# Time mixing with a SoLU expert on one core: w in pairs, w_out in place, halves added before their column sums, masks first, and a second instruction order

## Chip, cores and metric

One core of a Trainium2 chip. The metric is the device time of one execution in microseconds (us); lower is better. Every run is an execution of the whole kernel. An execution that is over 1.5% above the fastest of its kernel counts as slow and is left out of the ratios. A profile belongs to one execution; its span, from the first instruction recorded to the last, is about 1.8 us shorter than the time of that execution.

## The reference

The first half is a recurrence over time with a state of 48 x 48 per head; the second half takes its output, token by token, through two matrices with an exp-weighted activation and a layer norm between.

```python
# r, k, v, w: (4, 8, 768, 48) f32;  u: (8, 48)
for t in range(S):
    cur = einsum('bhd,bhe->bhde', u * k[t], v[t])
    y[t] = einsum('bhd,bhde->bhe', r[t], state + cur)
    state = w[t][..., None] * state + einsum('bhd,bhe->bhde', k[t], v[t])
x = y as (3072, 384)
h = x @ w_in                       # (3072, 1024)
e = exp(h - max(h));  solu = h * e / sum(e)
ln = (solu - mean) / sqrt(var + 1e-6) * g_ln
out = ln @ w_out                   # (3072, 384)
```

## The kernel before

The work is cut into 24 units of 128 tokens (6 chunks of time for each of 4 batches). A unit passes through some forty stages, each a short function. One long list, `ORDER`, says in which order the stages of all units are written into the program: the word `es13v` is stage `es` of unit 13 on VectorE (`a` ScalarE, `v` VectorE, `g` GpSimd). Each engine runs its own words strictly in the order of that list, so a word that waits holds up every later word of its engine.

Names that matter: `ldw ldk ldr ldv` load, `lw` is log w, `cum` its cumulated sums, `H` the hidden product, `e` its exp, `he` = h e, `hq` = (h e) squared, `Oa` and `Ob` the halves of the output product, `sq qm lv rs` the small chain that makes the norm's factor, `o` the scaled output, `sto` its store. `dm` are filler matmuls. SBUF is the core's working memory; PSUM is the memory that TensorE's results go to, and tiles that end in `_ps` lie there. To evict a tile is to copy it out of PSUM.

```python
# loads: one unit, one tensor, 192 KB
t = io.tile([C, H, 64], F32, tag=name + "_in", ...)            # 7 buffers
sp.dma_start(out=L[name], in_=src[b, :, c * C:(c + 1) * C, :].rearrange("h t d -> t h d"))
...
def log_w(i):
    act.activation(out=L["lw"][:, :, :D], in_=L["w"], func=LN)
...
# w_out: gains into gw, then the mean of the rows subtracted into w2
engine.tensor_scalar(out=gw[:, f, :], in0=wout_f[:, f, :], scalar1=gr[:, f:f + 1], op0=MULT, ...)
engine.tensor_add(out=w2[:, f, :DM], in0=gw[:, f, :], in1=mean_sb)
...
def output(i, part):               # o_ps: (128, 387), columns 385 and 386 are the two sums
    for f in range(part * KF // 2, (part + 1) * KF // 2):
        pe.matmul(o_ps[:, :DM + 1], lhsT=he[:, f, :], rhs=w2[:, f, :], ...)
        pe.matmul(o_ps[:, DM + 1:DM + 2], lhsT=e[:, f, :], rhs=inv_col, ...)
    if part == 1:
        for f in range(KF):        # KF = 8
            pe.matmul(o_ps[:, DM + 2:], lhsT=L["hq"][:, f, :], rhs=one_col, ...)
...
L["o"] = io.tile([C, DM], F32, tag="o", name="o", bufs=5)
```

The end of its list, from unit 23's x on:

```text
X23 qm19 lv19 hq20g o19a xT22v e21 xT23v H22 e22 he21 Ob20 sto18 hq21g sq20a qm20 lv20 H23 he22 Oa21
Oa22 sto19 Ob21 e23 hq22g sq21a o20v qm21 lv21 Ob22 he23 hq23v Oa23 sto20 sq22v sq23a qm22 o21v Ob23
sto21 lv22 qm23 Oc23 o22v sto22 lv23 dm14 oz23v dm15 o23a stz23 dm7 sto23 dm11 dm19
```

The softmax here doesn't subtract the row's maximum and nothing guards it: scores larger than these inputs give would overflow.

## Time and profile before

| | time, us |
|---|---|
| median of the first three runs | 151.97 (151.48 to 153.03) |
| the execution that was profiled (slow) | 156.91, span 155.2 |
| a later profile (`before_again`) | 151.62, span 149.8 |

The profile fell into a slow execution; the prediction below reads that one, and it infers that a fast execution has almost no idle time of TensorE after 35 us. The second profile was taken with the experiments.

### The profile page before, as it was taken

What the parts mean: (1) busy time and instruction counts of PE and PEld (TensorE: products, weight loads), DVE (VectorE), ACT (ScalarE), POOL (GpSimd) and SP (SyncE); (2) the same over time, 40 slices, a digit from 0 to 9 for tenths busy, and PEclk for the clock granted to TensorE, in tenths of its full rate; (3) what the DMA queues carried; (4) which work ended last, traced back from release to release, by engine and by line L of the source; (5) the groups of instructions that cost most, each with busy time, mean ns of one, the idle gap of its engine ahead of it and who ended that gap; (6) DMA issues with size and microseconds to landing.
All of it is one profiled execution on the core that took longest, in us unless ns stands there. A gap on an engine that the chain in (4) does not pass through costs nothing.

```text
span 155.2 us, 5295 instructions
## 1 busy us (share of the span) xinstructions
PE 140.4 (90%) x2156; PEld 109.7 (71%) x2156; DVE 129.4 (83%) x231; ACT 120.2 (77%) x232; POOL 123.1 (79%) x152
## 2 busy tenths in 40 slices
PE   6877897699999899999999799939999999999993
PEld 2344584477786787888788587737888778889771
DVE  7546738899998898999976989999889999998661
ACT  4456767989898979798989698829899888895742
POOL 3375965997999799999947999977799899976800
PEclk9999999999999999999999999999999999999999
DMA  4999997989999999899796999999989311011013
GB/s 95 201 185 301 380 303 152 213 160 190 208 202 184 204 229 187 194 205 233 154 205 157 218 217 200 228 250 180 215 196 211 100 51 55 2 55 55 18 62 127
DMA packets 104970, 27.09 MB, mean 175 GB/s; under 512 B 100329, under 2 KB 104562, under 8 KB 104946
## 3 DMA queue, kind: packets, MB, share of 16 engines
q1 hardware_dynamic: 104946, 26.75, 76.4%
q8 instruction: 17, 0.28, 0.7%
q14 instruction: 7, 0.06, 0.1%
HBM read 22.03 MB, written 4.72 MB: 172 GB/s over the span
## 4 chain that ended last, share of the span: by engine, by line
PE 50%; DMA 14%; DVE 10%; SPq 8%; POOL 8%; ACT 4%; issue 3%; POOLq 0%; DVEq 0%
PE o_ps L71 18%; PE h_ps L71 13%; SPq L71 8%; DMA kr_in<-in_k_dram 8%; DMA wout_f<-in_moe_w_out_dram 6%; POOL w L71 5%; PE kr_ps L71 5%; PE cum_ps L71 3%; PE m_ps L71 3%; PE y_ps L71 3%; PE s_ps L71 3%; DVE hq L71 3%; DVE kp L71 2%; PE x_ps L71 2%; DVE he L71 1%
## 5 line engine op out<-in xcount | busy, mean ns | idle before, releaser
L71 PE MATMUL o_ps<-w,he 128*128 128x385 bf16 (+2 forms) x200 | 42.2, 315 | 0.3 <-ACT sq L71 0.3
L71 PE MATMUL h_ps<-xT,win_sb 128*128 128x128 bf16 x576 | 36.0, 219 | 0.1
L71 PEld LDWEIGHTS <-win_sb 128*128 128x128 bf16 x576 | 32.9, 98 | 0.9 <-issue 0.2
L71 PE MATMUL o_ps<-inv_col,e 128*128 128x1 bf16 x192 | 31.1, 165 | 0.0
L71 DVE TENSOR_TENSOR he<-h_ps,e 128x1024 bf16<-128x1024 f32 x24 | 29.2, 1217 | 2.2 <-ACT e L71 2.2
L71 POOL TENSOR_TENSOR hq<-he 128x1024 bf16<-128x1024 bf16 x14 | 26.5, 1895 | 3.7 <-DVE he L71 2.4
L71 ACT ACTIVATE e<-h_ps 128x1024 bf16<-128x1024 f32 x24 | 24.5, 1021 | 6.2 <-PE h_ps L71 6.1
L71 PEld LDWEIGHTS <-he 128*128 128x128 bf16 x208 | 19.7, 96 | 10.5 <-issue 0.3
L71 ACT ACTIVATE cum_ps<-cum_ps 128x772 f32<-128x772 f32 (+1 forms) x24 | 19.2, 801 | 8.8 <-PE cum_ps L71 7.6
L71 DVE TENSOR_TENSOR kp<-cum_ps,kr_in 128x768 bf16<-128x768 f32 x24 | 22.7, 948 | 0.6 <-DMA kr_in<-in_r_dram 0.5
L71 POOL TENSOR_TENSOR q<-p,u_bc 128x384 bf16<-128x384 bf16 x23 | 22.0, 962 | 0.6 <-DVE p L71 0.5
L71 POOL TENSOR_TENSOR p<-kr_in 128x384 bf16<-128x384 f32 x18 | 17.9, 1001 | 5.4 <-DMA kr_in<-in_k_dram 5.4
L71 PEld LDWEIGHTS <-kp 128*128 128x128 bf16 x272 | 17.6, 102 | 4.4 <-DVE kp L71 2.3
L71 POOL TENSOR_TENSOR dv<-vb,dg 128x384 bf16<-128x384 bf16 x22 | 18.2, 830 | 2.3 <-ACT vb L71 1.5
L71 DVE TENSOR_TENSOR m<-m_ps,uts 128x1024 bf16<-128x1024 f32 x14 | 17.0, 1223 | 3.1 <-PE m_ps L71 3.0
L71 PEld LDWEIGHTS <-e 128*128 128x128 bf16 x192 | 18.3, 96 | 0.1
L71 PE MATMUL kr_ps<-ident,kp 128*128 128x128 bf16 x192 | 15.9, 230 | 1.4 <-DVE kp L71 1.4
L71 PEld LDWEIGHTS <-kr 64*128 64x128 bf16 (+1 forms) x272 | 10.7, 98 | 4.9 <-DVE kr L71 2.2
L71 ACT ACTIVATE lw<-w_in 128x384 bf16<-128x384 f32 x23 | 11.7, 523 | 2.7 <-DMA w_in<-in_w_dram 2.7
L71 ACT COPY kr<-kr_ps 128x1024 bf16<-128x1024 bf16 x13 | 13.2, 1014 | 0.5 <-PE kr_ps L71 0.4
L71 POOL TENSOR_SCALAR_AFFINE_SELECT m<-m 128x1024 bf16<-128x1024 bf16 x10 | 11.0, 1103 | 2.5 <-ACT m L71 2.4
L71 PE MATMUL cum_ps<-lw,uti_neg 128*128 128x384 bf16 x24 | 8.3, 347 | 4.8 <-DVE kp L71 3.3
(93 smaller groups left out, 284.3 us busy)
## 6 DMA issues: line engine op xcount, KB each, us to landing
w_in<-in_w_dram SPq DMA_DIRECT2D x24, 192.0 KB, 4.2
kr_in<-in_r_dram SPq DMA_DIRECT2D x24, 192.0 KB, 3.8
kr_in<-in_k_dram SPq DMA_DIRECT2D x24, 192.0 KB, 3.8
v_in<-in_v_dram SPq DMA_DIRECT2D x24, 192.0 KB, 3.8
out_dram<-o SPq DMA_DIRECT2D x23, 192.0 KB, 3.1
win_f<-in_moe_w_in_dram SPq DMA_DIRECT2D x3, 512.0 KB, 6.1
wout_f<-in_moe_w_out_dram SPq DMA_DIRECT2D x2, 768.0 KB, 8.8
out_dram<-o SPq DMA_DIRECT2D x2, 96.0 KB, 1.6
```

The costliest lines, as they stand in the source:

```text
L71: made = make(*args, **kwargs)
```

## The change

The intent: fewer instructions (w of two units loaded and logged at once from unit 4 on; half of the one-column matmuls of some units replaced by one addition of halves), less memory (w_out scaled in place), an earlier identity mask, and a list in a second order that fits the new durations. The queue of loads is nearly as it was. Cut to its core:

```diff
+ t2 = io.tile([C, 2, H, 64], F32, tag="w_in", name="w_in", bufs=4)          # load, name == "w"
+ if i >= 4:
+     sp.dma_start(out=L["w2_in"]..., in_=src[b:b + 2, :, c * C:(c + 1) * C, :]...)
- act.activation(out=L["lw"][:, :, :D], in_=L["w"], func=LN)
+ act.activation(out=<both units of t>, in_=<both units of w2_in>, func=LN)   # i >= 4
- engine.tensor_scalar(out=gw[:, f, :], in0=wout_f[:, f, :], ...)
+ engine.tensor_scalar(out=w2[:, f, :DM], in0=wout_f[:, f, :], ...)
- engine.tensor_add(out=w2[:, f, :DM], in0=gw[:, f, :], in1=mean_sb)
+ engine.tensor_add(out=w2[:, f, :DM], in0=w2[:, f, :DM], in1=mean_sb)
+ def halves(name, of):                     # es from e, hs from hq; 12 uses
+     t = L[name] = wk.tile([128, KF // 2, C], BF16, tag=name, name=name, bufs=2)
+     engine.tensor_add(out=t, in0=L[of][:, :KF // 2, :], in1=L[of][:, KF // 2:, :])
+ hq = L.get("hs", L["hq"]);  n = hq.shape[1]           # 4 matmuls where halves were added, else 8
+ # the sums of the second half of e are now a word of their own, Oe, left out where es exists
+ # masks: uti_neg, ident, uts, ident_f in one loop ahead of all else on GpSimd
```

The list is written anew in full. Its end now reads:

```text
X23 sto17 lv19 e22 xT23v es21v o19a Oa20 hq21a H23 Oa21 he22 e23 Ob20 es22v Oa22 hq22v hs22g sq20a
sto18 hs21v he23 Ob21 qm20 lv20 Ob22 hq23v sto19 o20a Oa23 Ob23 sq21v qm21 sto20 sq22v lv21 qm22 o21v
sq23a qm23 lv22 sto21 o22v Oc23 lv23 oz23v sto22 o23a stz23 sto23 dm10 dm2
```

## The prediction

> **What bounds the kernel now.** I read the page first: busy time of each engine (part 1) and its slices (part 2).
>
> ```profile
> PE 140.4 (90%) x2156; PEld 109.7 (71%) x2156; DVE 129.4 (83%) x231; ACT 120.2 (77%) x232; POOL 123.1 (79%) x152
> PE   6877897699999899999999799939999999999993
> DMA  4999997989999999899796999999989311011013
> ```
>
> TensorE (PE) is the fullest engine; the DMA engines are full up to about 120 us of the 155.2 us span and then nearly idle. So loads or matmuls are the bound, and the table of stretches says which:
>
> ```profile
> 0.00:35.00 35.00, 27.66 (x267) 17.85 (x267) 24.39 (x68) 23.15 (x31) 23.68 (x36) 1.00 0.92 221
> 35.00:53.00 18.00, 17.55 (x298) 14.22 (x295) 16.29 (x28) 15.90 (x35) 16.45 (x24) 1.00 0.97 197
> 53.00:81.00 28.00, 27.62 (x465) 22.56 (x466) 25.63 (x41) 24.44 (x51) 24.91 (x35) 1.00 0.97 202
> 81.00:104.00 23.00, 19.23 (x327) 15.77 (x326) 20.35 (x27) 16.88 (x35) 21.42 (x22) 1.00 0.94 211
> 104.00:122.00 18.00, 17.75 (x303) 14.38 (x301) 16.82 (x31) 16.37 (x31) 14.48 (x15) 1.00 0.93 203
> 122.00:151.00 29.00, 28.74 (x497) 24.08 (x494) 25.35 (x40) 22.35 (x50) 22.13 (x23) 1.00 0.10 37
> ```
>
> (Columns: stretch and length, busy us of PE, weight loads, DVE, ACT, POOL, then the granted clock, DMA share, GB/s.) From 35 us on PE idles 0.45, 0.38, 3.77, 0.25 and 0.26 us: 5.1 of 116 us, three quarters of it in one stretch. When the loads end (122 us), PE still has 29 us of backlog, more than five of the 24 units. So after the start the end is set by PE's total work. Before 35 us the loads set the pace.
>
> Third, the chain that ended last, for what filled the bad stretch and the start:
>
> ```profile
> 13.97 9.87 DMA wout_f<-in_moe_w_out_dram
> 26.75 7.75 POOL w L71 x8
> 98.33 4.01 DVE hq L71
> 125.12 0.73 PE o_ps L71 x8
> 126.65 0.93 PE o_ps L71 x16
> ```
>
> (Start, us, what.) The start waits for w_out, then for POOL's eight w2 passes. At 98 us one DVE square takes 4 us. The last two lines are used below. The profiled run took 156.91 us and is marked slow; the median is 151.97. The 4.9 us between them is about the 5.1 us of idle after 35 us, so in the fast runs PE should have almost none left there. That is an inference from one profile, but it decides my size: a new order has little idle time to win back.
>
> **What the Trainium skill says.** (1) "SBUF — State Buffer", section "Who interferes with whom": a DVE instruction with two SBUF inputs contends with a GpSimd instruction that reads SBUF, and the one that comes second blocks fully. The trace agrees. Of DVE's five squares four take about 0.69 us and one 4.09 us, and that one began while POOL went through q, dv, p, p without a gap:
>
> ```profile
> L71 DVE TENSOR_TENSOR hq<-he x5: 680/692/4091, 40.9 to 148.2; 128x1024 bf16<-128x1024 bf16 x5
> L71 DVE TENSOR_TENSOR p<-kr_in x5: 560/797/1837, 28.2 to 133.2; 128x384 bf16<-128x384 f32 x5
> ```
>
> (2) "TensorE: Matmul & The Clock Gate", section "Back-to-back issue gap": a matmul of 1 to 64 columns costs about 25 ns of issue. The chain agrees: the second half of an output has eight one-column matmuls more than the first and takes 0.93 against 0.73 us, so 25 ns each. The 165 ns that the groups show for one is latency, not cost. (3) "DMA: Bandwidth & Descriptors", section "Specifications": under 512 B per run the DMA loses its line rate. The trace agrees: 100329 of 104970 packets are under 512 B and the load-bound stages move about 200 GB/s, while the slices with the weights reach 380. (4) "ScalarE: Activation LUTs", section "What ACT_TABLE_LOAD costs": an ACTIVATE costs a fixed part plus 0.833 ns per element. The trace: 523 ns for 384 elements of lw, 1021 ns for 1024 of e from PSUM, so about 0.2 us are fixed.
>
> **The change, part by part.** *w in pairs:* ten pairs for units 4 to 23 replace twenty loads and twenty logarithms. The runs in DRAM stay 48 floats, 192 B, so packets and bytes stay as they are; by the packet argument the loads gain nothing, they only need ten issues fewer on a queue that was not short. The second w of a pair now comes up to one load (about 1 us) ahead of a k, r or v that is needed sooner. ACT: a pair costs an estimated 523 + 384 x 0.833 = 843 ns in place of 1046, so 10 x 0.2 = 2.0 us less. The rest of ACT's list moves by counts of the two orders times the durations of the groups: fewer m (3 x 1.01), w_out gains (3 x 0.6), w_in copies (1.05), v casts (2 x 0.5) and the mean copy (0.47); more squares (3 x 1.07), kr (3 x 1.01), y (4 x 0.48), o (2 x 0.58). Net with the pairs about -1 us: 119 us, not a bound.
>
> *w_out in place:* no work less, only 6 KB per partition for the larger w tiles. One of eight w2 passes goes from POOL to DVE, so the 7.75 us block becomes about 6.8 us.
>
> *Halves added:* the sum of e (units 4, 13, 19 to 22) and of hq (11, 15, 19 to 22) uses four matmuls in place of eight: 48 matmuls x 25 ns = 1.2 us off PE, 0.8 us of it in the last four of these units, where PE is the bound. The price is twelve adds of 512 elements: six on DVE (an estimate of half a 0.69 us square plus fixed cost, 0.43 us) and six on POOL (half of 1.89, about 1 us).
>
> *Bonus through PE:* nine units in place of five add dv by a matmul of 384 columns; the chain shows 0.53 us for such a y and 0.37 without, so 4 x 0.16 = +0.64 us on PE. Four fillers (dm) fewer lie in idle time. **PE in sum: -1.2 + 0.64 = -0.6 us.**
>
> *Masks first:* the identity was built only after p of unit 0, which waited 4.07 us for its k. That frees the first transposes by about 1 us, but the first hidden product waits for w_in (its last copy ended at 20.0, the product began at 20.06). The same loads still precede w_out, so w_out should land at 23.9 again. I give this 0.
>
> *Second order:* up to the first output PE's list has the same real stages before and after. The end is the same too, apart from where the halves save. DVE without blocking gains m (3 x 1.22), p (3 x 0.56), halves (6 x 0.43), gains, mean copy and w2 (about 1.9) and some; it loses kr (3 x 0.68), y (4 x 0.55), squares (2 x 0.69), o (2 x 0.61) and others: net about +3.3 us. POOL: six halves, two bonus halvings and two v casts more; three p, three masks and four centrings less: about -1 us. DVE instructions with two SBUF inputs go from 13 to 21 (p 8, q 2, dv 1, squares 3, halves 6, w2 1). Over what they take unblocked, the 13 lost about 6 us, half of it in the one 4.09 us square; without it about 0.2 us each. So some 1.8 us of blocking more on DVE. DVE then stands near 134 us, second to PE; most of it lies beside PE work.
>
> **Sum.** 151.97 - 0.6 (PE) - 0.6 (my choice: part of the shorter w2 block reaches PE) + 0.3 (my choice: DVE blocking that PE feels) = 151.1; I say 151.0.
>
> **Rivals.** *A: the order does more than the arithmetic.* If fast runs still hold the idle time of 81 to 104 us, and the new order has none, 3 to 4 us go: 147.5 to 148.5. For it: the chain has two waits of over 4 us for a k load at 39.7 and 46.5, and a DVE p of unit 9 that stood in line for the second; the new order puts that p on POOL. Against: PE idles only 0.45 us from 35 to 53, so those waits cost PE next to nothing. *B: DVE becomes the bound.* 8 more exposed instructions, each able to wait through a gapless run of POOL; one wait like the 4.09 us square on the path costs PE about 2.7 us, as at 100 us. Two of them: 155 to 157. Against: six of the eight more lie at the start or the end (p of 0 to 2, halves of 21 and 22), where POOL has gaps. *C: the paired loads starve a stage.* 1 us more per pair in front of a k while DMA is at 0.97: +1 to 2 us, 152.5 to 153. Against: PE's backlog of five units hides it after 60 us.
>
> **Range and chances.** The PE sum alone allows 1 us; over 2% (below 148.93) needs rival A. Above 155.0 needs B more than once, or B with C. I take 148.3 to 154.2; faster 0.17, within 2% 0.70, slower 0.13.
>
> **What would show it right or wrong.** Right: PE from 35 us on again with about 1 us or less of idle outside one or two stalls, PE busy near 140 less warm-ups, w_out landing at about 23.9, loads ending near 122, the backlog then about 28 us, lw pairs at about 0.84 us, halves at 0.43 (DVE) and 1.0 us (POOL). Wrong: PE finishing more units by 35 us or loads ending well before 118 us (the start or the DMA got faster, against my packet argument), or new waits of PE on DVE two-input instructions of over 1.5 us.

## The result, and the profile after

| | runs | median us (range) | ratio to before, 95% interval |
|---|---|---|---|
| before | 5 | 151.97 (151.48 to 153.03) | |
| changed | 5 | 153.95 (153.24 to 154.16) | 1.0116 [1.0068, 1.0164] |

A ratio here is the mean time of one kernel's fast runs over the mean of the other's fast runs of the same rounds, so it is not quite the ratio of the medians. The changed kernel is 1.2% slower. That is inside the predicted range and inside "within 2%", but the forecast was a gain of 0.6%, so the sign was wrong.

The table of stretches of the fast execution of the old kernel, then of the changed one (columns as in the prediction: stretch, length, busy us of TensorE, its weight loads, VectorE, ScalarE, GpSimd, then granted clock, DMA share, GB/s):

```profile
35.00:53.00 18.00, 17.31 (x295) 13.94 (x293) 16.64 (x28) 15.91 (x35) 16.41 (x24) 1.00 0.97 196
53.00:81.00 28.00, 28.00 (x474) 22.89 (x473) 25.67 (x40) 24.42 (x51) 26.74 (x37) 1.00 0.96 203
81.00:104.00 23.00, 23.00 (x397) 19.14 (x396) 21.36 (x39) 20.57 (x43) 22.35 (x22) 1.00 0.96 215
104.00:122.00 18.00, 17.76 (x304) 14.51 (x302) 16.66 (x27) 16.09 (x30) 16.64 (x18) 1.00 0.84 189
```

```profile
35.00:53.00 18.00, 18.00 (x319) 14.86 (x317) 17.16 (x31) 16.46 (x32) 16.69 (x23) 1.00 0.98 204
53.00:81.00 28.00, 28.00 (x474) 22.84 (x471) 25.12 (x43) 25.10 (x50) 27.02 (x30) 1.00 1.00 203
81.00:104.00 23.00, 21.97 (x367) 17.78 (x365) 22.13 (x37) 19.59 (x38) 20.86 (x25) 1.00 0.99 218
104.00:122.00 18.00, 18.00 (x300) 14.87 (x298) 16.40 (x29) 15.82 (x33) 17.46 (x18) 1.00 0.74 174
```

The old kernel idles 0.93 us on TensorE in these 87 us, so the prediction's inference about fast executions holds. The changed kernel has won that back (no idle time in three stretches) and has lost 1.03 us in a new place, between 81 and 104 us. So the middle alone does not explain a loss of 1.8 us. To find the rest I cut each span at two points: the start of `e2` (the exp of unit 2, when the loads stop setting the pace) and the end of TensorE's last matmul that is not a filler. Both are read from the timelines.

| profile (us) | e2 starts | e2 to TensorE's end | TensorE's end to the end | span |
|---|---|---|---|---|
| before | 34.84 | 111.33 | 3.63 | 149.8 |
| changed | 35.96 | 111.03 | 4.91 | 151.9 |
| difference | +1.12 | -0.30 | +1.28 | +2.1 |

The prediction had -0.3 us for the middle (-0.6 of TensorE, +0.3 of blocking), -0.6 us for the start (the shorter pass over w_out) and nothing for the end. The middle shows -0.30 us, but by luck: it holds losses of 1.2 and 0.8 us, shown below, that the prediction did not have, and so also gains that it did not have. The start and the last microseconds cost 2.4 us together. All this is one profile of each kernel. The two starts of `e2`, old and changed:

```profile
34.84 1.02 ACT L71 ACTIVATE e<-h_ps 128x1024 bf16<-128x1024 f32 x1
35.96 1.02 ACT L72 ACTIVATE e<-h_ps 128x1024 bf16<-128x1024 f32 x1 [0.31 <-PE h_ps L72]
```

**The stall at 97 us.** The timelines of VectorE, GpSimd and TensorE of the changed kernel (start, length, engine, line, operation, out<-in; at the end the idle time before it and who ended it):

```profile
95.75 0.94 DVE L72 TENSOR_TENSOR kp<-cum_ps,kr_in 128x768 bf16<-128x768 f32 x1
96.61 1.98 DVE L72 TENSOR_TENSOR es<-e 128x512 bf16<-128x512 bf16 x1
98.52 0.55 DVE L72 TENSOR_TENSOR y<-y_ps,dv 128x384 bf16<-128x384 f32 x1
```

```profile
96.42 1.89 POOL L72 TENSOR_TENSOR hq<-he 128x1024 bf16<-128x1024 bf16 x1
```

```profile
97.72 0.32 PE L72 MATMUL o_ps<-w,he 128*128 128x385 bf16 x1
98.65 0.18 PE L72 MATMUL o_ps<-inv_col,es 128*128 128x1 bf16 x1 [0.61 <-DVE es L72]
...
100.84 0.32 PE L72 MATMUL cum_ps<-lw,uti_neg 128*128 128x384 bf16 x1 [0.42 <-DVE he L72]
```

`es13`, an addition of halves, has both inputs in SBUF. GpSimd's `hq13` began 0.19 us before it and ended at 98.31; `es13` ended at 98.59. The other three `es` on VectorE took 415 or 416 ns. GpSimd was idle at the start of two of them (51.38 and 140.43 us) and within 0.12 us of the end of an instruction at the start of the third (138.67 us):

```profile
L72 DVE TENSOR_TENSOR es<-e x4: 415/416/1977, 51.4 to 140.4; 128x512 bf16<-128x512 bf16 x4
```

So an instruction that removes four matmuls of 25 ns took two microseconds, and TensorE waited for it (0.61 us) and for what stood behind it in VectorE's list (0.42 us).

**The end.** VectorE from the exp of unit 23 on, first the old kernel, then the changed one:

```profile
141.51 1.22 DVE L71 TENSOR_TENSOR he<-h_ps,e 128x1024 bf16<-128x1024 f32 x1 [0.55 <-ACT e L71]
142.84 0.69 DVE L71 TENSOR_TENSOR hq<-he 128x1024 bf16<-128x1024 bf16 x1
```

```profile
142.09 0.93 DVE L72 TENSOR_TENSOR hs<-hq 128x512 bf16<-128x512 bf16 x1 [0.64 <-PE o_ps L72]
142.95 1.21 DVE L72 TENSOR_TENSOR he<-h_ps,e 128x1024 bf16<-128x1024 f32 x1
144.19 0.69 DVE L72 TENSOR_TENSOR hq<-he 128x1024 bf16<-128x1024 bf16 x1
```

The exp of unit 23 ended at 141.48 in the old kernel and at 141.58 in the changed one, yet the product `he23`, on which the whole last output depends, began 1.44 us later. In front of it in VectorE's list stands `hs21`, which waited 0.64 us for a buffer and then took 0.93 us. `hs` has two buffers; in program order `hs22` comes before `hs21`, so `hs21` takes the buffer of `hs20`, which `Ob20` reads, and the new order puts `Ob20` behind the last hidden product on TensorE. The 0.93 us are a second collision of the kind of `es13`: GpSimd had begun `hs22` half a microsecond earlier. Undisturbed, as in `hs21_first` below, `hs21` takes 0.42 us.

```profile
141.59 1.15 POOL L72 TENSOR_TENSOR hs<-hq 128x512 bf16<-128x512 bf16 x1 [1.49 <-DVE hq L72]
```

The chain that ended last names the pieces on VectorE:

```profile
140.46 1.51 PE o_ps L72 x16
142.09 0.93 DVE hs L72
143.02 1.15 DVE he L72
144.19 0.35 DVE hq L72
```

A second loss follows. In the old list `sq23a` stands before `Ob23`, in the new one after it. Both touch the same PSUM tile, so the small chain of the last unit's norm (`sq`, `qm`, `lv`, `rs`) starts after the matmuls of `Ob23`. ScalarE at the end of the old kernel and of the changed one:

```profile
144.46 0.17 ACT L71 ACTIVATE sq<-o_ps 128x2 f32<-128x2 f32 x1 [0.43 <-PE o_ps L71]
...
146.40 0.42 ACT L71 ACTIVATE o<-o_ps,rs 128x192 f32<-128x192 f32 x1
```

```profile
146.37 0.17 ACT L72 ACTIVATE sq<-o_ps 128x2 f32<-128x2 f32 x1 [0.85 <-PE o_ps L72]
...
147.70 0.42 ACT L72 ACTIVATE o<-o_ps,rs 128x192 f32<-128x192 f32 x1
```

TensorE was done at 146.17 and 146.99: the last eviction on ScalarE begins 0.23 us after that in the old kernel and 0.71 us after it in the changed one. That is 0.48 of the 1.28 us. The changed list also evicts unit 22 on VectorE only at 147.28 us, so three stores and not two follow at the very end: the last store is issued at 148.8 us, against 147.3 us in the old kernel.

### The profile page after: what moved, and what is told of

Its sections match the earlier page's. It is cut to its first block, busy times and chain, and to the rows that moved or that the text cites. A ratio compares the mean times of both kernels' runs of the same rounds, so it can differ in the third digit from the quotient of the medians.

```text
span 151.9 us, 5187 instructions
## 1 busy us (share of the span) xinstructions
PE 137.1 (90%) x2106; PEld 107.9 (71%) x2108; DVE 130.7 (86%) x241; ACT 120.5 (79%) x223; POOL 123.0 (81%) x146
## 4 chain that ended last, share of the span: by engine, by line
PE 67%; SPq 15%; DVE 8%; DMA 3%; issue 3%; ACT 2%; DVEq 0%
PE o_ps L72 22%; PE h_ps L72 19%; SPq L72 15%; PE kr_ps L72 6%; PE y_ps L72 5%; PE cum_ps L72 4%; PE m_ps L72 4%; PE s_ps L72 4%; DMA kr_in<-in_r_dram 3%; PE x_ps L72 2%; DVE he L72 2%; DVE kp L72 2%; DVE p L72 1%; ACT e L72 1%; DVE hs L72 1%
## 5 line engine op out<-in xcount | busy, mean ns | idle before, releaser
L72 PE MATMUL o_ps<-w,he 128*128 128x385 bf16 (+2 forms) x200 | 40.5, 316 | 0.0
L72 POOL TENSOR_TENSOR hq<-he 128x1024 bf16<-128x1024 bf16 x13 | 24.6, 1893 | 1.3 <-DVE he L72 0.9
L72 POOL TENSOR_TENSOR q<-p,u_bc 128x384 bf16<-128x384 bf16 x22 | 20.4, 926 | 5.6 <-DVE gr L72 5.4
L72 DVE TENSOR_TENSOR m<-m_ps,uts 128x1024 bf16<-128x1024 f32 x17 | 20.7, 1220 | 1.9 <-PE m_ps L72 1.7
L72 ACT COPY kr<-kr_ps 128x1024 bf16<-128x1024 bf16 x16 | 16.2, 1013 | 2.4 <-PE kr_ps L72 2.2
L72 PE MATMUL o_ps<-inv_col,e 128*128 128x1 bf16 x144 | 16.1, 165 | 0.0
L72 PE MATMUL m_ps<-kr 64*128 64x128 bf16 x192 | 10.0, 229 | 1.8 <-ACT kr L72 1.1
L72 POOL TENSOR_SCALAR_AFFINE_SELECT m<-m 128x1024 bf16<-128x1024 bf16 x7 | 7.7, 1098 | 4.9 <-ACT m L72 4.6
L72 ACT ACTIVATE o<-o_ps,rs 128x384 f32<-128x384 f32 (+1 forms) x19 | 10.8, 570 | 0.6 <-DMA out_dram<-o 0.3
L72 DVE TENSOR_TENSOR st<-s_ps,et 128x384 bf16<-128x384 f32 x20 | 10.9, 548 | 0.1
```

The lines of the kernel that those rows point to most:

```text
L72: made = make(*args, **kwargs)
```

## The experiments

Twelve runs, one of them the old kernel again, were made in three batches, each batch on one chip with its own runs of the old kernel (medians 151.58, 151.53 and 151.32 us). All gave correct results. The table has all of them, and the changed kernel from its own, earlier batch. The medians are over all executions, slow ones too; the ratios are over fast ones alone. Ratios of different batches compare less well than those of one. The columns after the ratio cut each profile as above, in us. The profiles of `tail_fixed` and `no_es13` fell into slow executions (granted clock 0.82 and 0.83) and are not used.

| kernel | median us | ratio [95%] | e2 | middle | end | span |
|---|---|---|---|---|---|---|
| `before_again` | 151.62 (one run) | | 34.84 | 111.33 | 3.63 | 149.8 |
| changed | 153.95 | 1.0116 [1.0068, 1.0164] | 35.96 | 111.03 | 4.91 | 151.9 |
| `hs21_first` | 152.76 | 1.0064 [1.0015, 1.0113] | 35.23 | 111.57 | 4.90 | 151.7 |
| `no_halves` | 152.38 | 1.0001 [0.9941, 1.0061] | 34.88 | 110.10 | 4.52 | 149.5 |
| `new_code_old_order` | 152.63 | 1.0069 [1.0027, 1.0111] | 35.82 | 111.17 | 3.81 | 150.8 |
| `tail_fixed` | 152.94 | 1.0028 [0.9962, 1.0094] | | | | |
| `start_fixed` | 154.08 | 1.0154 [1.0095, 1.0213] | 35.84 | 112.93 | 4.83 | 153.6 |
| `both_fixed` | 152.36 | 1.0043 [0.9993, 1.0094] | 35.28 | 110.63 | 4.09 | 150.0 |
| `old_order_single45` | 152.33 | 1.0027 [0.9980, 1.0074] | 36.01 | 111.42 | 3.67 | 151.1 |
| `no_es13` | 152.14 | 1.0045 [1.0018, 1.0073] | | | | |
| `no_es13_tail` | 151.90 | 1.0019 [0.9972, 1.0065] | 37.22 | 109.39 | 4.19 | 150.8 |
| `no_halves_tail` | 152.12 | 1.0044 [1.0013, 1.0075] | 34.89 | 110.80 | 3.71 | 149.4 |
| `order_only_tail` | 152.17 | 1.0047 [1.0015, 1.0078] | 35.52 | 110.90 | 3.58 | 150.0 |

### First batch: the end, the halves, the order

**The old kernel once more**, unchanged, for a profile of a fast execution.

> The kernel before, unchanged, for a profile of it in the fast state (the one at hand was slow, 156.9 us). Theory T (tail): the changed kernel loses its time after the last hidden product: from the exp of unit 23 to the end the changed profile has 11.4 us (140.56 to 151.9). I expect about 9.3 us here as in the slow profile, with the exp of units 0 to 22 within 0.7 us of the changed kernel's. Rival S (steady part): the exp of unit 22 is over 1.5 us earlier here than the 138.2 us of the changed kernel, and the tail is not shorter. Span about 150.3 us, and if the inference of the prediction holds, PE idle from 35 us to the last output under 1.5 us.

Measured: 151.62 us, and the idle time shown above. It confirms what the prediction had only inferred. Theory T holds for the tail (9.34 us) and for the exp of unit 22 (138.16 us against 138.23), but the exp of unit 2 is 1.12 us earlier than in the changed kernel, not within 0.7 us.

**hs21 moved ahead of hs22**, so that it takes the buffer of `hs19`, which has long been read:

```diff
- es22v Oa22 hq22v hs22g sq20a sto18 hs21v he23
+ es22v Oa22 hq22v hs21v hs22g sq20a sto18 he23
```

> The changed kernel with one word of the order moved ahead of another: the half sum of unit 21's squares takes its buffer before that of unit 22, so it reuses the buffer of unit 19 (long free) and not that of unit 20, which the output of unit 20 reads until after the last hidden product. No engine's own order changes. Theory T: the DVE wait of 0.64 us before it goes, the product he of unit 23 starts at about 0.8 us after its exp ends and not 1.4, and 0.5 to 0.8 us go from the time: ratio to the kernel before about 1.007. Rival S: no change, 1.011 to 1.012.

Measured: ratio 1.0064, and `he23` began 0.12 us after the exp of unit 23 ended, against 1.37 us in the changed kernel and about 0.8 us in theory T, which did not know of the collision:

```profile
141.97 0.42 DVE L72 TENSOR_TENSOR hs<-hq 128x512 bf16<-128x512 bf16 x1
142.31 1.22 DVE L72 TENSOR_TENSOR he<-h_ps,e 128x1024 bf16<-128x1024 f32 x1
```

The one word removes the wait and the collision together, because now `hs22` waits for the buffer of `hs20` and begins only at 142.70 us; the run does not separate the two. From the start of that exp to the end of the span it took 10.53 us, against 11.34. The mechanism is shown in the profile and is worth 0.8 us; the end stays longer than the old kernel's 9.34 us. (0.77 us of that difference is the work of `Ob20`, which the new order runs after the exp of unit 23 and the old one before it; without halves it is 0.94 us. This is why the table cuts at TensorE's end.)

**No halves**, all twelve taken out, eight sums each again:

```diff
- es4v ... hs11g ... es13v ... hs15v ... es19g hs19g es20g hs20g es21v es22v hs22g hs21v
+ Oe4 ... Oe13 ... Oe19 ... Oe20 ... Oe21 ... Oe22            # sums over the full e and hq
```

> The changed kernel without any of the twelve half sums (units 4, 11, 13, 15, 19 to 22); everything else as it is. By the matmul count of the prediction alone PE has 48 small matmuls more, 1.2 us: 155.1 us, ratio 1.02. Theory T: the half sums cost more than they save (wait of DVE in the tail, 2 us block of the one of unit 13, PE idle 0.6 us there and 0.5 us in the tail): 153.3 to 154.0, ratio 1.007 to 1.012.

Measured: ratio 1.0001. Both theories missed in the same direction: 48 matmuls more on the engine that sets the end, and the ratio falls by 1.1% of the old time. The profile has no idle time of TensorE between 35 and 122 us. From the exp of unit 14 to that of unit 15 it takes 7.81 us, against 9.05 in the changed kernel; no other step between units 2 and 23 differs by more than 0.2 us. Of the halves only `es13` lies between these two steps, so it costs 1.24 us in the middle, more than the 1.03 us of visible idle time.

**The new code in the old order** (pairs, w_out in place, masks, no halves):

```diff
- ORDER = the new list
+ ORDER = the old list; odd ldw and lw from unit 5 on left out, mean as meanA meanB, Oe<i> ahead of each Ob<i>
```

> All code of the change except the halves (w in pairs, w_out in place, masks first), with the order of the kernel before: each pair is loaded and logged where its first half was. Rival S (a feature costs, for example the paired loads): 153 to 155 us, ratio 1.01 or more. Theory T (the features are near free and the order with its tail costs): 151.5 to 152.8, ratio 0.997 to 1.005.

Measured: ratio 1.0069, between the two theories. The middle and the end are as in the old kernel within 0.2 us; the difference of its profile is in the start (35.82 against 34.84).

### Second batch: repairing the end and the start

**The end in the old order**, with `hs21` early:

```diff
- es22v Oa22 hq22v hs22g sq20a sto18 hs21v he23
+ es22v Oa22 hq22v hs21v hs22g sq20a sto18 he23
- Oa23 Ob23 sq21v qm21 sto20 sq22v lv21 qm22 o21v sq23a qm23 lv22 sto21 o22v Oc23 lv23 oz23v sto22 o23a
+ Oa23 sq21v qm21 sto20 sq22v lv21 sq23a qm22 o21v Ob23 sto21 lv22 qm23 Oc23 o22v sto22 lv23 oz23v o23a
```

> The changed kernel's code, with only the last instructions set in another order: the eviction hs21 ahead of the load of head 22's g, and after Oa23 the old kernel's sequence, in which sq23a comes before Ob23. Theory T (the end lost 2.0 us against the old kernel by the late hs21 and by the late scaling chain): end 9.4 to 9.9 us after the exp of unit 23 starts, against 11.35; ratio to the kernel before 0.998 to 1.004. Rival (the end is only a consequence of what went before it, so that the time lost shows up elsewhere): ratio 1.008 to 1.013, as without the edit.

(Where this text speaks of an eviction and of a load of head 22's g, `hs21` and `hs22g` are meant, two additions of halves.) Measured: 1.0028, in the range of theory T, but its interval [0.9962, 1.0094] reaches into the rival's. Its own profile was slow; `both_fixed` and `no_es13_tail` have the same end and take 4.09 and 4.19 us from TensorE's end on, against 4.91. From the exp of unit 23 on they take 10.12 and 10.21 us, not the 9.4 to 9.9 of theory T, which had left out the moved work of `Ob20`. Against the 10.53 us of `hs21_first` the second repair is thus worth 0.3 to 0.4 us, and not the 0.7 to 0.8 us of the last column: with `sq23a` first, TensorE waits 0.26 us for it before `Ob23`, in the old kernel too, and so ends later.

**The start**: w of units 4 and 5 single again, two squares of ScalarE later:

```diff
- if i >= 4:        # load and log in pairs
+ if i >= 6:
- ... he1 dm9 Y2x mean_sb:v hq0a hq1a ldk5 ... et3 ... Oa1
+ ... he1 dm9 Y2x mean_sb:v ldk5 ... et3 hq0a ... Oa1 hq1a       # ldw5 after ldk4, lw5 after exp4
```

> The changed kernel, with w of units 4 and 5 loaded and logged singly again (pairs from unit 6), and the scaling hq0a and hq1a on ScalarE put after the exp of unit 3 and after Oa1. Theory T (the first pair delays cum4 while TensorE has no backlog yet): the exp of unit 2 starts about 1 us earlier than in the changed kernel (near 35.0 us), cum4 waits under 0.5 us, ratio 1.003 to 1.007. Rival (the start's delay is hidden by the later backlog): ratio 1.009 to 1.013.

Measured: 1.0154, above even the rival's range, so the theory fell. Half of it did happen: TensorE's wait for log w of unit 4 went from 1.34 us

```profile
29.05 0.32 PE L72 MATMUL cum_ps<-lw,uti_neg 128*128 128x384 bf16 x1 [1.34 <-ACT lw L72]
```

to 0.49 us, but another wait took its place, and `e2` began at 35.84 instead of 35.96:

```profile
27.89 0.32 PE L72 MATMUL cum_ps<-lw,uti_neg 128*128 128x384 bf16 x1 [0.49 <-ACT lw L72]
29.64 0.56 PE L72 MATMUL kr_ps<-ident,kp 128*128 128x128 bf16 x7 [0.78 <-DVE kp L72]
```

Its profile also shows a stall of another kind, 2.3 us at 73 us, that I had overlooked in the profile of `hs21_first`. The waits of ScalarE between 68 and 77 us, and between 66 and 76 us for the other:

```profile
ACT o L72 <- DMA out_dram<-o: 2.3, 1, 2.3
```

```profile
ACT o L72 <- DMA out_dram<-o: 1.8, 1, 1.8
```

The eviction `o7` waits for the store of `o2` to land: `o` has five buffers. In the old list `sto2` stands 119 words before `o7`; in the new one 17, while the other stores up to unit 17 keep 33 words and more. Whether `o7` waits depends on how fast that one store gets through the loads. Of the seven usable profiles with the new order and the new code, the wait is 0.3 us in the changed kernel, 1.8 and 2.3 us in these two, and absent in `no_halves`, `both_fixed`, `no_es13_tail` and `no_halves_tail`; `order_only_tail` has 0.4 us. No profile in the old order has it. No kernel with an earlier store was measured: that it costs time in those two executions is shown (TensorE idles 0.97 us in `hs21_first` and 1.53 us in `start_fixed` between 53 and 81 us, and nothing there in the changed kernel), what it adds to the mean is open.

**Both repairs.**

```diff
+ the edits of tail_fixed and of start_fixed
```

> Both edits together. If the two losses add, as theory T has it: ratio 0.990 to 0.997. If either is hidden by the other or by something later: 0.998 to 1.006.

Measured: 1.0043, as the rival had it. The end is repaired; the start brings nothing against `tail_fixed` (1.0028) of the same batch. Its TensorE still idles 1.03 us between 81 and 104 us, for `es13`.

**The old order with w of units 4 and 5 single**, the new code otherwise:

```diff
- if i >= 4:        # load and log in pairs
+ if i >= 6:        # and ldw5 after ldk4, lw5 after exp4 in the old list
```

> The changed kernel's code in the old kernel's order, with w of units 4 and 5 single (pairs from unit 6). Theory T (its 0.7 us of loss come from the first pair): ratio 0.998 to 1.003, exp of unit 2 within 0.3 us of the old kernel's. Rival (they come from w_out in place or the masks' place): ratio stays at 1.005 to 1.009.

Measured: 1.0027 [0.9980, 1.0074], where theory T had 0.998 to 1.003. Yet its profile does not show the mechanism: `e2` began at 36.01, not within 0.3 us of 34.84, although TensorE's wait for log w of unit 4 fell from 2.26 us in `new_code_old_order` to 1.31 us. The intervals of this kernel and of `new_code_old_order` overlap. I take this as not settled.

### Third batch: es13, and the order by itself

**es13 left out**, one instruction:

```diff
- e14 ldr19 sto8 es13v Y15 ... et17 kp17 cum18 vb16g o11a Ob13
+ e14 ldr19 sto8 Y15 ... et17 kp17 cum18 vb16g o11a Oe13 Ob13
```

> The changed kernel with one instruction less: es13, the halves of unit 13's exp on VectorE, is left out, and TensorE sums that unit's e with eight columns instead of four (+0.1 us of TensorE). In every profile with es13 the exp of unit 15 comes 9.04 us after that of unit 14; without any halves it comes 7.81 after. Theory T (this one eviction of 1.98 us, slow beside GpSimd's hq13, holds VectorE's list and through it TensorE): 7.7 to 8.0 us, no wait of TensorE over 0.2 us between 81 and 104 us, ratio to the kernel before 1.002 to 1.006. Rival (the stall only moves to the next wait): 7.8 us there but the exp of unit 23 no earlier against that of unit 2 than 104.6 us, ratio 1.009 to 1.014.

Measured: 1.0045 [1.0018, 1.0073], as theory T had it, with four matmuls more on TensorE. What T said of TensorE's waits is read from the next run, because this one's profile was slow. Against the changed kernel that is 0.7%, or 1.1 us; the batches differ, so this compares two ratios, not two times on one chip.

**es13 left out and the end repaired.**

```diff
+ the edits of no_es13 and of tail_fixed
```

> The same, and the end in the order of tail_fixed (hs21 earlier, sq23a ahead of Ob23). Theory T (es13 costs 1.2 us, the end's order 1.3, and the two add): ratio 0.992 to 0.998. Rival (they hide each other): 0.999 to 1.006.

Measured: 1.0019 [0.9972, 1.0065], in the rival's range; theory T's 0.992 to 0.998 is missed, though the interval touches it. Here is its VectorE around the place, and its table row:

```profile
97.01 0.94 DVE L72 TENSOR_TENSOR kp<-cum_ps,kr_in 128x768 bf16<-128x768 f32 x1
98.38 0.56 DVE L72 TENSOR_TENSOR y<-y_ps,dv 128x384 bf16<-128x384 f32 x1 [0.42 <-PE y_ps L72]
```

```profile
81.00:104.00 23.00, 23.00 (x396) 18.77 (x394) 21.49 (x37) 20.82 (x39) 21.89 (x25) 1.00 1.01 226
```

VectorE now waits for TensorE, not TensorE for VectorE; the idle 1.03 us are gone, and from the exp of unit 14 to that of unit 15 it is 7.81 us. The middle is 109.39 us, 1.94 less than the old kernel's and the shortest of all. In this profile the start takes it back: `e2` began at 37.22 us. Whether the start does so in the mean is not shown. Its runs spread from 150.59 to 152.57 us, the old kernel's ten fast ones of this batch from 151.11 to 151.88.

**No halves, the end in the old order.**

```diff
+ the edit of no_halves
- Oa23 Ob23 sq21v qm21 sto20 sq22v lv21 qm22 o21v sq23a qm23 lv22 ...
+ Oa23 sq21v qm21 sto20 sq22v lv21 sq23a qm22 o21v Ob23 sto21 lv22 ...
```

> No halves at all, and the end in the old kernel's order (sq23a ahead of Ob23). Without halves the exp of unit 23 came 103.87 us after that of unit 2, against 105.62 in the old kernel. Theory T (the order wins that 1.75 us, the end's order gave it back): end 9.3 to 9.9 us after the exp of unit 23, ratio 0.988 to 0.995. Rival (the end is set by other things than the order of its last instructions): end 10.6 to 10.9, ratio 0.998 to 1.003.

Measured: 1.0044, a miss of theory T. The end was repaired (3.71 us after TensorE's end, against 4.52), but in the profile TensorE itself ended 0.7 us later relative to `e2` than in `no_halves`, part of it a new wait of 0.3 us of `Ob23` for `sq23a`. Also, my 1.75 us was wrongly counted: it ended at the exp of unit 23, before `Ob20`, whose 0.94 us of work only moved. Cut at TensorE's end, the order without halves wins 0.5 to 1.2 us (110.80 and 110.10 against 111.33). With intervals of 0.3 and 0.6%, the runs do not tell `no_halves` and `no_halves_tail` apart.

**The old code in the new order**, no halves, the end in the old order:

```diff
- ORDER = the old list, in the old kernel
+ ORDER = the list of no_halves_tail; ldw<i+1> and lw<i+1> behind each ldw<i> and lw<i> from unit 4 on, one mean, no Oe
```

> The old kernel's code (w single, w_out and its scaled copy apart, old masks), in the new order without halves and with the old end. Theory O (the order alone wins the 1.75 us): exp of unit 23 about 103.9 us after that of unit 2, ratio 0.988 to 0.996 and within 0.003 of no_halves_tail. Rival (the order needs the paired loads and the shorter pass over w_out that came with it): ratio 0.997 to 1.01.

Measured: 1.0047, within 0.0003 of `no_halves_tail`. So pairs, w_out in place and masks neither help nor hurt by more than about 0.4%, which the two intervals leave open, once the order is given, as theory O had it; but the order alone is not faster than the old one, as theory O did not have it. Its profile shows why a little: the middle is 0.43 us shorter, the start 0.68 us longer.

### The start

In the fast profiles with the new order, `e2` began at 34.88, 34.89, 35.23, 35.28, 35.52, 35.84, 35.96 and 37.22 us. Five of these (all but 35.28, 35.52 and 35.84) come from programs whose instructions are the same up to there, so the same instructions scatter by 2.3 us (35.23 to 37.22 us among the three that hold halves). The old kernel has 34.84 us in one fast profile and 36.17 us in the slow one.

The granted clock does not sort them: over the first 35 us it was 0.80 in the profile with 34.84 us, 1.00 with 35.96 us and 0.95 with 37.22 us. Nor does the landing of w_out: the engine that waits for its second half went on at 22.08, 24.13 and 22.93 us in these three.

The mean over the new order is 35.6 us, 0.8 us above the old kernel's single fast value, and the kernels whose middle and end together are shorter than the old one's (`no_halves`, `both_fixed`, `no_es13_tail`, `no_halves_tail`, `order_only_tail`) still have ratios above 1.

Part of that lies outside the profile. The time is 1.70 to 1.79 us longer than the span in the mean of most kernels' fast runs, but 1.92 and 1.95 us in `no_halves` and `no_halves_tail` and 2.14 us in `order_only_tail`; nothing says why. By spans alone (mean of the fast runs over that of the old kernel in the batch) these three have ratios of 0.999, 1.003 and 1.002. What is left points at a start that costs a few tenths of a per cent on average, but with one fast profile of the old kernel it is an inference.

The wait for log w of unit 4 is not new. The old kernel has it as well (first line); in the old order the pair makes it longer (second line, `new_code_old_order`), and `e2` does not follow, since it began at 35.82 us with the pair and at 36.01 us without:

```profile
27.61 0.32 PE L71 MATMUL cum_ps<-lw,uti_neg 128*128 128x384 bf16 x1 [1.31 <-ACT lw L71]
27.89 0.32 PE L72 MATMUL cum_ps<-lw,uti_neg 128*128 128x384 bf16 x1 [2.26 <-ACT lw L72]
```

New in the changed kernel are two waits before it, 0.69 us and 0.99 us, of the mean of w_out's rows for gains on GpSimd; the profiles in the old order have none. The last gain to end is now one on GpSimd, which took 1.47 us. No run moved it back, so what it costs is not known.

```profile
25.65 0.82 PE L72 MATMUL mean_ps<-w,mean_w 128*128 128x384 bf16 x4 [0.99 <-POOL w L72]
```

What bounds the start in the changed kernel is visible in its chain of what ended last:

```profile
23.90 0.63 SPq L72
24.57 4.32 DMA kr_in<-in_r_dram
28.98 0.96 DVE kp L72
```

A load of r is on the path, issued after a wait of the load queue. In `start_fixed` the chain between 22 and 34 us runs over VectorE's products and ScalarE's copies, a square among them, and no load. So several chains seem to end there at nearly the same time, and removing one wait exposes the next; that is a reading of two profiles.

## Why the prediction was right or wrong

The measured 153.95 us lies inside the range, 0.25 us below its upper end, and that is no support for the sum behind it: the gain of 0.9 us did not come, and the loss arose at places where the sum had a gain, +0.3 or nothing.

- **"In the fast runs PE should have almost none left there."** Right: 0.93 us of idle time between 35 and 122 us in a fast profile.
- **PE in sum -0.6 us.** The gain was set too small: the middle shows -0.30 us with the stalls of `es13` and `hs21` in it and -1.94 us in the one profile of `no_es13_tail` without them. The halves and the new order together could have won more than I gave them.
- **The halves' price.** This step failed. I priced an addition at 0.43 us on VectorE and put it "beside PE work". Of the six on VectorE, three took 0.415 us, as said; `es13` took 1.98 us, `hs21` 0.93 us and `hs15` 0.68 us, all three begun well inside an instruction of GpSimd. Of `es13`, 1.24 us came through to the exp of unit 15. On GpSimd they took 1.15 to 1.24 us, against 1.0 predicted. I had cited the very rule for two SBUF inputs beside GpSimd and had even counted 21 exposed instructions. But I turned them into an average of 0.2 us each, and gave the sum +0.3 us, instead of asking of each new one what GpSimd does at that moment. The list answers it: `hq13g` stands five words behind `es13v`. Rival B had the mechanism; I set it aside because six of the eight new instructions lie where GpSimd has gaps. But the eight are a net count, eleven that came less three that went, and of the eleven `es4`, `es13` and `hs15` are halves in the middle. Even among the six, `hs21` met `hs22`, another addition of the same change. My own sign for it, a wait of TensorE of over 1.5 us, did not show: the waits were 0.61 and 0.42 us. The list alone does not decide, either: the old kernel's square of 4.09 us in the slow profile took 0.68 us in the fast one, while `es13` took 1.98 us in every fast profile that has it.
- **"The end is the same too, apart from where the halves save."** This step failed outright. I compared which stages stand in TensorE's list, not which buffers and tiles they share. `hs21` behind `Ob20` through a buffer and `Ob23` ahead of `sq23` through a tile made the end 1.28 us longer after TensorE's end and delayed `he23` by 1.4 us before that. The profiles show both repaired: from the exp of unit 23 to the end 11.34 us, 10.53 us with the first repair, 10.1 to 10.2 us with both. The ratios go the same way, 1.0116, 1.0064 (`hs21_first`) and 1.0028 (`tail_fixed`), but their intervals overlap. Within a batch, the repair of the end takes `start_fixed` from 1.0154 to 1.0043 and `no_es13` only from 1.0045 to 1.0019, so its size in the mean is not settled.
- **Rival A**, that the order wins idle time back: it does (no idle time in `no_halves` from 35 to 122 us), but 0.4 to 1.2 us, not 3 to 4. Its condition failed: the fast execution has no idle time between 81 and 104 us.
- **Rival C**, that paired loads starve a stage: no stage after 60 us starved. At unit 4, where there is no backlog, TensorE waits 1.34 us for log w, but 1.31 us in the old kernel too, and shortening the wait won nothing in the new order. `new_code_old_order` (1.0069) against `old_order_single45` (1.0027) points at 0.4% for the first pair, without being settled.
- **Masks first, 0, and w_out in place, 0 but for GpSimd's seven passes.** `order_only_tail` against `no_halves_tail` (1.0047, 1.0044) agrees that they and the pairs together do not matter within about 0.4% in the new order; in the old order the same code has 1.0069. The 0.6 us that I gave the shorter pass over w2 failed: GpSimd's pass fell from 7.82 us to 6.28 us, but it began 0.86 us later, and `e2` came no earlier. That w_out should land "at 23.9 again" came true (24.1 us), but 23.9 was the slow profile's time; in the fast one it is 22.1 us.
- **Sizes.** The paired logarithm took what was said, 0.84 us:

```profile
L72 ACT ACTIVATE lw<-w_in 128x768 bf16<-128x768 f32 x10 | 8.5, 846 | 0.1
```

VectorE rose by 3.5 us with its blocking (127.2 to 130.7), where I had 3.3 and 1.8 us of blocking more. The terms listed for ScalarE add up to about 0 and not to -1 us, because two copies of `xT` fewer are left out of the list; measured, ScalarE rose from 119.5 to 120.5 us. The loads fell off between 116 and 119 us in both fast profiles, not at 122, which I had read from the slow one.

What stays open: the mean cost of the start, whether the first pair or the later gains of w_out have a part in it, why the kernels without halves spend more time outside the span, and what the late store of `o2` adds to the mean. No kernel measured here beats the old one with certainty; `no_halves` (1.0001) and `no_es13_tail` (1.0019) come nearest, and the fastest runs of the latter (150.59, 150.61) lie below the fastest of the old kernel in that batch (151.11).

## What to carry to other kernels

When a list fixes the order on every engine, judge a new order not by which stages it holds but by what each word now stands behind: the buffer that it takes over, the tile that it shares, and the word in front of it on its engine. An instruction that saves 0.1 us on the busiest engine, like a half sum here, can cost 1.2 us where it collides; price it at its worst case at that very place, not at a mean. And cut profiles that you compare at a point with the same work behind it; about half of the 1.75 us that I took for a gain in `no_halves` was half an output product that had only moved.

## What the Trainium skill lacked or had wrong

- "SBUF — State Buffer", "Who interferes with whom": no run contradicts it, but it does not say what a collision costs a whole list of instructions. Here an addition of 0.415 us that began 0.19 us after a GpSimd square of 1.89 us took 1.98 us and ended 0.28 us after it; TensorE's work came 1.24 us later for it.
- No page that I read says how much the start of a load-bound kernel scatters: programs with the same instructions up to that point began the exp of unit 2 between 34.88 and 37.22 us in fast executions, more than most effects studied here.
- None that I read has it: how long a store takes that is issued among loads which fill the DMA engines. Here the store of `o2`, 192 KB, kept its buffer until 74.8 us, 5 us after it was issued at 69.8, and the eviction that needed the buffer waited 2.3 us for it (in `start_fixed`).
